# An mLSTM cell feeding a two-matrix block: first weight staged in unused activation columns, q scaling on GpSimd, tanh moved into the mix

## The chip, the core and the metric

The kernel runs on one core of one Trainium2 chip. The metric is device time in microseconds (us) of one execution. The five engines are TensorE (PE; its weight loads are shown as PEld), VectorE (DVE), ScalarE (ACT), GpSimd (POOL) and SyncE (SP, here the engine that issues nearly all transfers). Each runs its own list of instructions in order and waits for the others by semaphores.

## The reference

For 4 batches x 8 heads, a gated recurrent cell runs over 768 positions with head size 40. Its result is brought to 3072 tokens x 320, and goes through two matrices with a leaky ReLU between them:

```python
for t in range(S):
    m_new = np.maximum(f_gate[:, :, t] + m, i_gate[:, :, t])
    f_stab = np.exp(f_gate[:, :, t] + m - m_new)
    i_stab = np.exp(i_gate[:, :, t] - m_new)
    C = f_stab[..., None, None] * C + i_stab[..., None, None] * np.einsum('bhd,bhe->bhde', vt, kt)
    n = f_stab[..., None] * n + i_stab[..., None] * kt
    h_tilde = np.einsum('bhde,bhe->bhd', C, qt)
    denom = np.maximum(np.abs(np.einsum('bhd,bhd->bh', n, qt)[..., None]), 1.0)
    y[:, :, t] = sigmoid(o_gate[:, :, t]) * h_tilde / denom
x = y.transpose(0, 2, 1, 3).reshape(3072, 320)
h = x @ w_in                              # 320 x 2048
out = np.maximum(0.01 * h, h) @ w_out     # 2048 x 320
```

The two weights arrive as 64-bit floats; all else is float32.

## The kernel before, in words

**Chunks and steps.** Time is cut into six chunks of 128 positions. A step s handles one chunk of one batch, s = 4 x chunk + batch, so there are 24 steps. Inside a chunk the recurrence is a masked product: scores between the keys and queries of the chunk, weighted by gates, plus the state C carried from the chunk before.

**What a step does** (the letters in brackets are used in the prediction):

- `ahead(s)` prepares it. `prep_kq` (L398) transposes keys and queries on DVE into `kqT` (L403), and multiplies the queries by a decay `ea` (L409, two instructions of 40x512) into `qs`, which lies in the `kq` tile. `prep_mask` (L357) adds the causal mask to the 128x1024 tile `w` on POOL. `prep_exp` (L365) takes eight exponentials of `w` on ACT. `prep_vu` (L384) scales values on POOL. `prep_o` (L392) takes the tanh of the o gate on ACT.
- `u_scores(s)` (L432) multiplies keys and queries on PE; DVE multiplies the scores into `w` (L436).
- `u_mix(s)` updates the state and computes the output: PE writes `pT` from C and `qs` (L507) and from `w` and the values (L513); DVE transposes it into `hb` (L519), forms denominators, and multiplies by the gate (L523, which needs the tanh); POOL divides (L526); DVE adds to the state (L465) and transposes the result `x` (L530). The sync engine writes `x` to DRAM (L533) and `gather_x` reads it back in the layout that the matrix block needs (L547).

`ahead(s+1)` is emitted right after `u_scores(s)`, and `u_mix(s)` some units later.

**The matrix block.** While the steps of chunk c run, PE also multiplies the tokens of chunk c-1. Per chunk there are eight pairs: each writes two PSUM tiles `ph` with `w_in` (L576; 20 records in the trace for each pair, the first 12 from `first`, 8 from `second`), and ACT applies the leaky ReLU to both (L584), which also frees them. Then sixteen parts multiply by `w_out` (L611, 8 records each). For chunk 0 each pair is cut into two halves of 256 tokens. The tiles `ph` and the output tiles `po` come from one PSUM pool of four buffers, so a pair can only start when the ReLU of the pair two before it has read its tiles.

**Who sets the order.** PE, DVE, ACT and POOL run exactly in the order in which the Python code emits their instructions. A loop over the units of the matrix block (L761 to L791) puts the units of the steps between them. The sync engine's list is ordered by the scheduler of the framework, and each transfer also waits for the one that used its semaphore before: there are eight of these in turn, shared by the queues of SP and ACT.

**Weights.** Each of the eight blocks of the two weights (n = 0 to 3 for `w_in`, 4 to 7 for `w_out`) lands as 64-bit words in a `raw` tile of a pool with two buffers and is then narrowed: an Abs on ACT (L209) and six instructions on DVE (L211 to L227). Block 0 has no `raw` tile: it lands in the last columns of `acts`, the tile of the activations, which chunk 0 does not fill until later. The o gates of the first four steps lie in such columns too.

**Chunk 1** is the stage where the narrowing of blocks 2 to 7, the steps of chunk 1 and the matrix block of chunk 0 run together: `todo` (L751) says at which unit i the narrowing of each block starts; `lead` (L758) delays the first scores to i = 11.

Of the kernel before, what the change touches and what calls it, by code (L numbers as in the profile page):

```python
# [11 lines left out]
U64 = mybir.dt.uint64  # L12
# [6 lines left out]
def kernel(  # L19
# [26 lines left out]
    nc = tc.nc  # L46
# [5 lines left out]
    Dm, FF = moe_w_in.shape  # L52
# [9 lines left out]
    NF = FF // P  # L62
    GT = B * P
# [55 lines left out]
    acts_l = acts[:].rearrange("p f t -> p (f t)")  # L119
# [26 lines left out]
    QN = NF // 4  # L146
    QC = 4 * P
    WC = KC * 2 * P
# [12 lines left out]
    def run_of(r, at):  # L161

        ks = SLOTS[r][at:]
        return ks[0], next((i for i in range(1, len(ks)) if ks[i] != ks[i - 1] + 2), len(ks))
# [4 lines left out]
    def load_weights(n):  # L169

        if n < QN:
            dst = w_in[:, n, :]
        else:
            dst = w_out[:, 4 * (n - QN) : 4 * (n - QN + 1), :].rearrange("p a d -> p (a d)")
        to = dst
        if wide:
            if n == 0:
                raw = acts_l[:, NF * GT - 2 * WC :].bitcast(U64)
            else:
                raw = wk.tile([P, dst.shape[1]], U64, name="raw")[:]  # L180
            raws[n] = (raw, dst)
            to = raw
        if n < QN:
            for r in range(2):
                cols = slice(n * QC + 2 * P * r, n * QC + 2 * P * (r + 1))
                src = moe_w_in[:, cols].rearrange("(k p) c -> p k c", p=DP)
                half = to[DP * r : DP * (r + 1), :].rearrange("p (k c) -> p k c", k=KC)
                at = 0
                while at < KC:
                    k0, n_k = run_of(r, at)  # L190
                    nc.sync.dma_start(half[:, at : at + n_k, :], src[:, k0 : k0 + 2 * n_k - 1 : 2, :])  # L191
                    at += n_k
        else:
            rows = moe_w_out[(n - QN) * QC : (n - QN + 1) * QC, :]
            nc.sync.dma_start(to.rearrange("p (a d) -> p a d", d=Dm), rows.rearrange("(a p) d -> p a d", p=P))
# [101 lines left out]

    def load_o(s):
        c, b = divmod(s, B)
        at = NF * GT - 2 * WC - (s + 1) * Dm  # L300
        st[s]["o"] = acts_l[:, at : at + Dm]
        nc.sync.dma_start(
            st[s]["o"].rearrange("p (h d) -> p h d", d=D), o_gate[b, :, ts(c, P), :].rearrange("h p d -> p h d"),
        )
# [14 lines left out]
    def raw_blocks(s, i, w):  # L319

        return blocks(rb_t[s % NR][:, i, QW : QW + RL])[:, :, :w]
# [67 lines left out]
    def prep_o(s):  # L389

        o = st[s]["o"] if s < B else raw_blocks(s, 2, DB)
        nc.scalar.activation(o, o, AF.Tanh, scale=0.5)  # L392
# [5 lines left out]
    def prep_kq(s):  # L398

        d = st[s]  # L400
        d["kqT"] = wk.tile([P, 2, PR * P], F32, name="kqT")
        for i in range(2):
            nc.vector.transpose(  # L403
                in_blocks(d["kqT"][:, i]), raw_blocks(s, i, QW).rearrange("p (j n) d -> p j n d", n=TB),
            )
        d["qs"] = d["kq"][:, 1].rearrange("p h d -> p (h d)")
        for r in range(2):
            rows = slice(DP * r, DP * r + D)
            nc.vector.tensor_tensor(  # L409
                d["qs"][rows], d["kqT"][rows, 1], d["ea"][rows].rearrange("p j t -> p (j t)"), op=ALU.mult,  # L410
            )

# [85 lines left out]
    def u_mix(s):  # L498

        c, b = divmod(s, B)  # L500
        d = st[s]
        if c + 1 < NB:
            state(s)
        pT = psc.tile([P, PR * P], F32, name="pT", tag="c")
        for j in range(PR):
            for r in range(2):
                nc.tensor.matmul(  # L507
                    pT[DP * r : DP * (r + 1), ts(j, P)], lhsT=C[:, b, j, r, :], rhs=d["qs"][:, ts(j, P)],
                    start=True, stop=False,
                )  # L510
            for r in range(2):
                h = 2 * j + r
                nc.tensor.matmul(  # L513
                    pT[DP * r : DP * (r + 1), ts(j, P)], lhsT=d["va"][:, h], rhs=d["w"][:, h, :], start=False, stop=True,
                )
        if c + 1 < NB:
            state_scale(s)
        hb = wk.tile([P, PR * TB, QW], F32, name="hb", bufs=1)
        nc.vector.transpose(hb[:].rearrange("p (j n) d -> p j n d", n=TB), in_blocks(pT[:]))  # L519
        den = wk.tile([P, PR * TB], F32, name="den")  # L520
        denominators(den[:], hb[:, :, DB])
        x3 = xb[:, :, :DB]
        nc.vector.scalar_tensor_tensor(  # L523
            x3, in0=raw_blocks(s, 2, DB), scalar=1.0, in1=hb[:, :, :DB], op0=ALU.add, op1=ALU.mult,
        )
        nc.gpsimd.tensor_tensor(x3, x3, den[:].unsqueeze(2).to_broadcast([P, PR * TB, DB]), op=ALU.mult)  # L526
        if c + 1 < NB:
            state_add(s)
        xq = wk.tile([P, PR * P], F32, name="x")
        nc.vector.transpose(in_blocks(xq[:]), xb[:].rearrange("p (j n) d -> p j n d", n=TB))  # L530
        to = x_dr[s].rearrange("(j n i) t -> n i j t", n=4, i=DB)
        for n in range(4):
            nc.sync.dma_start(to[n], xq[QW * n : QW * n + DB].rearrange("p (j t) -> p j t", t=P))  # L533
        del st[s]

    def gather_x(s):

        c, b = divmod(s, B)
        if ("xT", c) not in st:
            st["xT", c] = wk.tile([P, KC, GT], F32, name="xT", bufs=1)  # L540
        xT = st["xT", c]
        src = x_dr[s].rearrange("(k p) t -> p k t", p=DP)
        for r in range(2):
            at = 0
            while at < KC:
                k0, n = run_of(r, at)
                nc.sync.dma_start(xT[DP * r : DP * (r + 1), at : at + n, ts(b, P)], src[:, k0 : k0 + 2 * n - 1 : 2, :])  # L547
                at += n
# [91 lines left out]
    def ahead(s):  # L640

        if s < NS:
            prep_kq(s)
            if s + NR < NS:
                load_blocks(s + NR, 0)
                load_blocks(s + NR, 1)
            prep_mask(s)
            prep_exp(s)
            prep_vu(s)
            prep_o(s)  # L650

    def feed(s):
        load(s)
# [80 lines left out]
    with tc.manual_schedule(engines={E.PE, E.DVE, E.Activation, E.Pool}):  # L734
        ffs = first_chunk()
        feed(B)
        for i in range(3):
            load_blocks(B, i)
        load_weights(QN)
        load_weights(QN + 1)  # L740
        feed(B + 1)
        for i in range(3):
            load_blocks(B + 1, i)
        load_weights(QN + 2)
        load_weights(QN + 3)
        feed(B + 2)
        feed(B + 3)


        ffs = ffs[4:6] + ffs[2:4] + ffs[6:]  # L750
        todo = {0: 2, 4: 3, **{9 + 4 * n: QN + n for n in range(4)}}  # L751
        now = iter(())
        for c in range(1, NB + 1):
            if c > 1:
                ffs = ff_units(c - 1)
            cells = cell_units(c) if c < NB else []
            n_ff, n_c = len(ffs), len(cells)
            lead = 10 if c == 1 else 0  # L758
            done = 0
            waiting = []  # L760
            for i in range(n_ff):  # L761
                if c == 1:
                    if i in todo:
                        for _ in now:
                            pass
                        now = narrow_weights(todo[i])
                    next(now, None)
                    next(now, None)
                    if i == 8:
                        u_gates(1)  # L770
                        ahead(B)
                if i == lead and c + 1 < NB:
                    bus[c + 1] = gates(c + 1)
                ffs[i]()
                upto = min(n_c, max(0, i + 1 - lead) * n_c // (n_ff - 6 - lead))
                while done < upto:
                    fn, s = cells[done]
                    fn(s)
                    done += 1
                    if fn is u_scores:  # L780
                        ahead(s + 1)
                    elif fn is u_mix:
                        waiting.append(s)
                        if s + NR < NS:
                            load_blocks(s + NR, 2)
                        if s + NL < NS:
                            feed(s + NL)
                if i >= n_ff // 2 - 1:
                    for s in waiting:
                        gather_x(s)  # L790
                    waiting.clear()  # L791


# [29 lines left out]
```

## Time and profile before

| | |
|---|---|
| time, median of 3 runs | 611.62 us (611.05 to 612.6) |
| span of the profiled execution | 611.2 us |
| PE busy | 545.6 us, 89% |
| DVE busy | 257.3 us, 42% |
| ACT busy | 154.9 us, 25% |
| POOL busy | 110.8 us, 18% |
| transfers | 69.89 MB, mean 114 GB/s |

PE is busy nine tenths of the span, so what counts is where it is not: before about 63 us, in chunk 1 (63 to 190 us), and shortly where one chunk follows another. From 190 us on each chunk takes about 87 to 90 us. In the timelines a bracket at the end of a line says how long the engine had been idle and what ended that; "issue" means that the profile shows no cause.

### The profile page before, as it was taken

Reading aid. Unit: us, or ns where it says so; the run is one execution under the profiler, and the core shown is the slowest. Engines: PE = TensorE matmul, PEld = TensorE weight load, DVE = VectorE, ACT = ScalarE, POOL = GpSimd, SP = SyncE. Lnnn points to the kernel's source line nnn. Section 1 sums busy time; section 2 is a strip of 40 time slices with the busy share of each in tenths; the row PEclk is TensorE's granted clock in tenths of the full one; section 3 lists DMA queues with packets and bytes.
Section 4 is the critical chain, followed back from the end, with each engine's and each line's share of the span. In section 5 each row is a group of like instructions: output and inputs, shape, how many; then the busy total and the mean of one; then the engine's idle time right before and its main releaser. Section 6 shows DMA issues by size and latency. Waiting matters only on the chain.

```text
span 611.2 us, 9093 instructions
## 1 busy us (share of the span) xinstructions
PE 545.6 (89%) x3428; PEld 375.2 (61%) x3428; DVE 257.3 (42%) x423; ACT 154.9 (25%) x401; POOL 110.8 (18%) x128
## 2 busy tenths in 40 slices
PE   5876992978655999998999989999989999999997
PEld 5765882756435656675557758557757567754575
DVE  4756796698830555242444423543503433100000
ACT  4443442420202332203321203330203330012100
POOL 4021520333020322130333020332100110000000
PEclk9998895999786999999999998999999999999999
DMA  9995588744574454661564660664650231100000
GB/s 141 169 170 125 122 254 188 177 159 106 137 174 125 108 137 129 151 157 59 139 149 117 153 160 11 149 144 122 153 146 25 71 92 38 48 23 1 0 23 21
DMA packets 158412, 69.89 MB, mean 114 GB/s; under 512 B 87072, under 2 KB 151200, under 8 KB 158368
## 3 DMA queue, kind: packets, MB, share of 16 engines
q1 hardware_dynamic: 157696, 69.08, 47.8%
q8 instruction: 27, 0.44, 0.3%
q10 hardware_dynamic: 672, 0.23, 0.2%
q14 instruction: 17, 0.14, 0.1%
HBM read 61.90 MB, written 7.37 MB: 113 GB/s over the span
## 4 chain that ended last, share of the span: by engine, by line
PE 72%; SPq 9%; DMA 6%; DVE 6%; issue 5%; ACT 1%; POOL 0%; ACTq 0%; DVEq 0%; POOLq 0%
PE ph L576 34%; PE po L611 28%; PE pT L513 3%; SPq L296 3%; PE pT L507 3%; SPq L314 3%; PE sc L432 3%; DMA rb<-in_k_dram 2%; SPq L191 1%; DVE kqT L403 1%; DVE kq L409 1%; PE dC L444 1%; DMA a_dr<-a 1%; DMA raw<-in_moe_w_in_dram 1%; SPq L331 1%
## 5 line engine op out<-in xcount | busy, mean ns | idle before, releaser
L576 PE MATMUL ph<-xT,w_in 64*128 64x512 f32 (+1 forms) x1120 | 228.0, 557 | 33.9 <-issue 16.3
L611 PE MATMUL po<-w_out,acts 128*128 128x320 f32 x768 | 214.8, 436 | 3.6 <-DVE w_out L227 3.6
L576 PEld LDWEIGHTS ph<-xT,w_in 64*128 64x128 f32 x1120 | 132.6, 199 | 113.1 <-issue 85.5
L611 PEld LDWEIGHTS po<-w_out,acts 128*128 128x128 f32 x768 | 143.5, 190 | 67.4 <-issue 6.0
L584 ACT ACTIVATE acts<-ph 128x512 f32<-128x512 f32 (+1 forms) x112 | 53.7, 532 | 160.7 <-PE ph L576 150.8
L436 DVE TENSOR_TENSOR w<-w,sc 128x512 f32<-128x512 f32 x48 | 30.7, 682 | 149.5 <-PE sc L432 149.5
L365 ACT ACTIVATE w<-w,gT 128x128 f32<-128x128 f32 x192 | 58.5, 394 | 17.5 <-POOL w L357 17.4
L455 POOL TENSOR_TENSOR C<-C,gL 64x168 f32<-64x168 f32 x32 | 15.8, 495 | 240.9 <-PE pT L507 239.7
L616 ACT COPY y<-po 128x320 f32<-128x320 f32 x24 | 10.2, 425 | 194.4 <-PE po L611 166.5
L357 POOL TENSOR_TENSOR w<-w,cmask 128x1024 f32<-128x1024 f32 x20 | 47.4, 2372 | 0.1
L513 PE MATMUL pT<-w,va 128*64 128x128 f32 x320 | 34.5, 280 | 8.2 <-issue 5.7
L403 DVE STREAM_TRANSPOSE kqT<-rb 128x512 f32<-128x512 f32 x40 | 41.1, 1105 | 0.0
L519 DVE STREAM_TRANSPOSE hb<-pT 128x512 f32<-128x512 f32 x20 | 14.3, 716 | 60.5 <-PE pT L513 60.5
L526 POOL TENSOR_TENSOR xb<-xb,den 128x320 f32<-128x320 f32 x20 | 14.6, 728 | 111.0 <-DVE xb L523 94.8
L507 PE MATMUL pT<-kq,C 128*64 128x128 f32 x320 | 34.0, 283 | 0.0
L432 PEld LDWEIGHTS sc<-kqT 40*128 40x128 f32 x384 | 28.4, 205 | 8.1 <-issue 7.4
L409 DVE TENSOR_TENSOR kq<-kqT,ea 40x512 f32<-40x512 f32 x40 | 29.4, 736 | 4.6 <-DMA ea<-a_dr 3.3
L432 PE MATMUL sc<-kqT 40*128 40x128 f32 x384 | 30.5, 297 | 0.0
L513 PEld LDWEIGHTS pT<-w,va 128*64 128x64 f32 x320 | 23.7, 141 | 9.4 <-issue 6.7
L530 DVE STREAM_TRANSPOSE x<-xb 128x512 f32<-128x512 f32 x20 | 22.4, 1120 | 8.3 <-POOL xb L526 8.3
L507 PEld LDWEIGHTS pT<-kq,C 128*64 128x64 f32 x320 | 21.8, 140 | 2.4 <-issue 2.0
L392 ACT ACTIVATE rb<-rb 128x320 f32<-128x320 f32 x20 | 9.3, 465 | 43.9 <-DMA rb<-in_o_gate_dram 39.9
(84 smaller groups left out, 278.7 us busy)
## 6 DMA issues: line engine op xcount, KB each, us to landing
w<-a_dr SPq DMA_DIRECT2D x20, 512.0 KB
rb<-in_k_dram SPq DMA_DIRECT2D x80, 80.0 KB
rb<-in_q_dram SPq DMA_DIRECT2D x80, 80.0 KB
rb<-in_o_gate_dram SPq DMA_DIRECT2D x80, 80.0 KB
ea<-a_dr SPq DMA_DIRECT2D x40, 128.0 KB
raw<-in_moe_w_out_dram SPq DMA_DIRECT2D x4, 1280.0 KB
kq<-in_k_dram SPq DMA_DIRECT2D x24, 160.0 KB
xT<-x_dr SPq DMA_DIRECT2D x40, 96.0 KB
```

The source lines that it names most:

```text
L357: nc.gpsimd.tensor_tensor(w[:], w[:], cmask[:].unsqueeze(1).to_broadcast([P, H, P]), op=ALU.add)
L365: nc.scalar.activation(w[:, h, :], w[:, h, :], AF.Exp, bias=gT[c][:, 0, bh : bh + 1], scale=1.0)
L403: nc.vector.transpose(in_blocks(d["kqT"][:, i]), raw_blocks(s, i, QW).rearrange("p (j n) d -> p j n d", n=TB),)
L409: nc.vector.tensor_tensor(d["qs"][rows], d["kqT"][rows, 1], d["ea"][rows].rearrange("p j t -> p (j t)"), op=ALU.mult,)
L432: nc.tensor.matmul(sc[r][:, j, :], lhsT=kqT[rows, 0, ts(j, P)], rhs=kqT[rows, 1, ts(j, P)], start=True, stop=True,)
L436: nc.vector.tensor_tensor(w[:, r::2, :], w[:, r::2, :], sc[r][:], op=ALU.mult)
L507: nc.tensor.matmul(pT[DP * r : DP * (r + 1), ts(j, P)], lhsT=C[:, b, j, r, :], rhs=d["qs"][:, ts(j, P)], start=True, stop=False,)
L513: nc.tensor.matmul(pT[DP * r : DP * (r + 1), ts(j, P)], lhsT=d["va"][:, h], rhs=d["w"][:, h, :], start=False, stop=True,)
L530: nc.vector.transpose(in_blocks(xq[:]), xb[:].rearrange("p (j n) d -> p j n d", n=TB))
L576: nc.tensor.matmul(ph[r][:, cols], lhsT=w_row(r, slot, j), rhs=xT[DP * r : DP * (r + 1), slot, cols], start=(slot == 0), stop=(slot == KC ...
L584: nc.scalar.activation(acts[:, f, cols], ph[r][:, cols], AF.Prelu, alpha=0.01)
L611: nc.tensor.matmul(po[n][:], lhsT=acts[:, f, ts(n, P)], rhs=w_out[:, f, :], start=(f == 0), stop=(f == NF - 1),)
```

## The change

Four edits:

1. Block 1 of the weights lands in unused columns of `acts` too, below block 0; the first o gates move further down. This leaves both `raw` buffers free for blocks 2 and 3 at once.
2. The loads of `w_out` (blocks 4 to 7) are no longer issued among the transfers of chunk 1's steps. Each is issued in the loop when the narrowing of the block before it starts, so that chunk 1's own transfers go ahead of them instead of waiting in one queue behind a load that waits for a buffer.
3. The tanh of the o gate moves from `ahead(s+1)` to the head of `u_mix(s)`, so that ACT does not stand waiting for a gate that is not needed yet. With it, `gather_x` is emitted before the transfers for later steps (`feed`, `load_blocks`).
4. The scaling of the queries by `ea` moves from DVE to POOL, which has more room.

```diff
         if wide:
-            if n == 0:
-                raw = acts_l[:, NF * GT - 2 * WC :].bitcast(U64)
+            if n < 2:
+                at = NF * GT - 2 * WC * (n + 1)
+                raw = acts_l[:, at : at + 2 * WC].bitcast(U64)
...
-        at = NF * GT - 2 * WC - (s + 1) * Dm
+        at = NF * GT - 4 * WC - (s + 1) * Dm
...
-            nc.vector.tensor_tensor(
+            nc.gpsimd.tensor_tensor(
                 d["qs"][rows], d["kqT"][rows, 1], d["ea"][rows].rearrange("p j t -> p (j t)"), op=ALU.mult,
             )
...
         d = st[s]
+        prep_o(s)
         if c + 1 < NB:
             state(s)
...
             prep_vu(s)
-            prep_o(s)
...
             load_blocks(B, i)
-        load_weights(QN)
-        load_weights(QN + 1)
         feed(B + 1)
...
             load_blocks(B + 1, i)
-        load_weights(QN + 2)
-        load_weights(QN + 3)
         feed(B + 2)
...
                         now = narrow_weights(todo[i])
+                        if QN - 1 <= todo[i] < 2 * QN - 1:
+                            load_weights(todo[i] + 1)
...
-                        if s + NR < NS:
-                            load_blocks(s + NR, 2)
-                        if s + NL < NS:
-                            feed(s + NL)
                 if i >= n_ff // 2 - 1:
                     for s in waiting:
                         gather_x(s)
                     waiting.clear()
+                while fed < done:
+                    fn, s = cells[fed]
+                    fed += 1
+                    if fn is u_mix:
+                        if s + NR < NS:
+                            load_blocks(s + NR, 2)
+                        if s + NL < NS:
+                            feed(s + NL)
```

More of the change, by code (lines that the diff above doesn't have):

```diff
@@ L758 @@
             lead = 10 if c == 1 else 0
-            done = 0
+            done = fed = 0
             waiting = []
@@ L783 @@
                         waiting.append(s)
+                if i >= n_ff // 2 - 1:
+                    for s in waiting:
+                        gather_x(s)
+                    waiting.clear()
+                while fed < done:
+                    fn, s = cells[fed]
+                    fed += 1
+                    if fn is u_mix:
                         if s + NR < NS:
@@ L787 @@
                             feed(s + NL)
[L788 to L791, printed above, removed]
 _INS = ['q', 'k', 'v', 'i_gate', 'f_gate', 'o_gate', 'moe_w_in', 'moe_w_out']
```

## The prediction, made before the changed kernel had run

> **What bounds the kernel now.** I read the busy shares first, then the waits, then the timeline of each engine where PE stands still. The shares say PE:
>
> ```profile
> PE 545.6 (89%) x3428; PEld 375.2 (61%) x3428; DVE 257.3 (42%) x423; ACT 154.9 (25%) x401; POOL 110.8 (18%) x128
> PEclk9998895999786999999999998999999999999999
> ```
>
> The second line is the granted clock in 40 slices of 15.3 us: it falls where PE had stood still. PE's timeline from 70 to 200 us shows the long holes, all in chunk 1:
>
> ```profile
> 104.62 6.44 PE L576 MATMUL ph<-xT,w_in 64*128 64x256 f32 x40 [12.00 <-ACT acts L584]
> ...
> 158.85 1.09 PE L513 MATMUL pT<-w,va 128*64 128x128 f32 x3 [5.70 <-issue]
> ...
> 189.54 9.26 PE L576 MATMUL ph<-xT,w_in 64*128 64x512 f32 x32 [13.67 <-issue]
> ```
>
> The first is ACT standing at the gate loads of L91, behind transfers queued late on SP; the second is ACT at a tanh whose o gate came late (15.76 us idle in front of it); the third is the last gather of x, issued late by SP. From 190 us on there are no holes but three at chunk boundaries (1.65, 2.63, 2.87 us). In a middle step (s = 9) the timelines of PE, ACT, POOL and DVE read:
>
> ```profile
> 215.86 6.18 PE L576 MATMUL ph<-xT,w_in 64*128 64x512 f32 x28
> 221.97 0.67 PE L444 MATMUL dC<-vu,kq 128*64 128x42 f32 x16
> 224.33 7.14 PE L576 MATMUL ph<-xT,w_in 64*128 64x512 f32 x32
> ```
>
> ```profile
> 213.56 2.44 ACT L365 ACTIVATE w<-w,gT 128x128 f32<-128x128 f32 x8
> 217.67 0.47 ACT L392 ACTIVATE rb<-rb 128x320 f32<-128x320 f32 x1 [1.67 <-DMA rb<-in_o_gate_dram]
> 218.05 1.07 ACT L584 ACTIVATE acts<-ph 128x512 f32<-128x512 f32 x2
> 222.07 1.09 ACT L584 ACTIVATE acts<-ph 128x512 f32<-128x512 f32 x2 [2.95 <-PE ph L576]
> ```
>
> ```profile
> 210.83 2.36 POOL L357 TENSOR_TENSOR w<-w,cmask 128x1024 f32<-128x1024 f32 x1
> ```
>
> ```profile
> 216.13 1.29 DVE L436 TENSOR_TENSOR w<-w,sc 128x512 f32<-128x512 f32 x2 [4.10 <-PE sc L432]
> 217.33 2.08 DVE L403 STREAM_TRANSPOSE kqT<-rb 128x512 f32<-128x512 f32 x2
> 219.44 1.40 DVE L409 TENSOR_TENSOR kq<-kqT,ea 40x512 f32<-40x512 f32 x2
> ```
>
> The reader should see that POOL masks w of step 10 at 210.8, before the scores of step 9 (215), so ACT's eight exponentials run at 213.6 and the ReLU at 218.05 follows its pair (8 records after 215.86, done at 217.6) at once. PE never waits for it.
>
> **The Trainium skill.** "GPSIMD Engine Reference", section 3.1, puts a two-input `tensor_tensor` at about 2.6 cycles an element, 4497 ns for 2048 elements; the trace agrees: the 128x1024 mask takes 2357 ns, 2.3 ns an element. "TensorE: Matmul & The Clock Gate", Part 1, says ScalarE, VectorE and GpSimd take their instructions strictly first in, first out, and that PE falls to half clock after an idle window of about 3.4 us, free-running. The trace agrees roughly: 32 records of L576 take 7.07 us; after the 1.65 us hole 7.21; after 2.63 us 10.38; after 2.87 us 40 records take 10.63 for 8.84.
>
> **The change part by part.**
>
> *Block 1 in `acts`.* Nothing: ACT's Abs of block 1 (48.1 us) has no wait in front of it before. Up to 82.4 us PE's order is the same and runs without a hole from 62.7; the o gates only change address.
>
> *q scaling on POOL.* Two 40x512 at 2.3 ns an element plus a little: 1.2 us each, 2.4 a step (DVE took 1.4). Bounds: 0.8 each at the page's best loop of 1.8 cycles, 1.35 if DVE contends (the 128x336 of L384 goes from 0.77 to 1.35). The sum, 48 us on an engine 18% busy, is no matter; the place is. In the built program POOL has: L409(s+1), mask(s+1), vu(s+1), then C(s), xb(s). L409(s+1) needs `kqT(s+1)`, which DVE makes after L436(s), which needs PE's scores of s. So the mask, independent of all this before, now waits for the scores. Behind the mask on ACT stand exp(s+1), and behind that the ReLUs; PE waits for those through the four PSUM buffers. At s = 9: DVE done 219.4; POOL 2.4 gives 221.9; mask 2.36, 224.2; exp 2.45, 226.7; ReLU of that pair frees its first tile at 227.2, the second at 227.7. The pair that needs these starts at 224.33 before: 3.1 us of standing. At s = 8 the same sum, from scores at 198.7 and kqT at 202.9, gives 210.7 to 211.2 against 208.0: 2.9 us. In chunks 2, 3 and 4 two steps each stand so (the third's ReLU is needed only in the last quarter of a part, some 12 us later, just in time): 6 x 3.0 = 18 us. In chunk 5 the scores stand a pair later; L409 to ReLU ends about 0.7 us late, twice: 1.4.
>
> *Clock.* Each such hole is about 2.8 us. Holes of that size cost 0.14, 3.3 and 1.8 us of slower matmuls on top; I take their mean, 1.75: 6 x 1.75 = 10.5. Ends: 0 and 3.3 each.
>
> *tanh in the mix.* ACT's tanh(s) now stands behind exp(s+1) and, in the middle steps, two ReLUs. DVE's L523 waits for it some 3 us, hidden, since the next thing that needs DVE is scores 6 us later. At chunk ends x is ready 2.5 us later, but its gather is issued right after the write and two loads, not behind eight transfers; the gather comes 0.2 to 1.4 us earlier than before: -0.5 a boundary, -1.5 for three.
>
> *Chunk 1 with the loads moved.* The transfers of step 5 are now there by 70 us, and the gate loads of L91 do not stand, so the 12.0 us hole goes. In its place: kqT(4) ends at 85.3 as before, then POOL 87.7, mask 90.1 (before: 70.9), exp 92.5, ReLU 93.1. PE has filled its four buffers at 87.1 and stands 6.0 us. Abs of block 4 moves from 86.5 to 93.1, and its narrowing with the gates of chunk 2 (8.5 us on DVE) ends at 103.1; L436(4), kqT(5) 106.4; POOL 108.8, mask 111.1, exp(5) 113.5, ReLU 114.1, and only then a buffer for the first part: 114.1 against 113.36 before. The 12 us are gone again. Going on with the same durations: L436(5) 124.5, L436(6) 139.2, kqT(7) 141.3, POOL's L409(7) 143.7. Now SP: its load of `ea` for step 8 waits for that L409. Behind it in the new order stand `ea`, a load, gather(4), write of x(5), gather(5) with its landing, and six or seven loads, about 13 us at 0.45 to 0.6 each, and then the load of the last `w_out` block: issued at about 157, before at 127.7. It lands in about 5 us (packets of the four before: 5 us each): Abs at 162.5 (before 152.7), four DVE instructions 4.1, L436(7) 169.3 (before 159.3). Then kqT(8) 171.4, POOL 173.8, `ea(9)` on SP, 12 us of issue to the write of x(7) at 186, its gather 189 to 191.6, PE about 194: 4.5 us later than 189.54. I take +5, ends -5 (the last block earlier) and +10.
>
> Sum: 5 + 18 + 10.5 + 1.4 - 1.5 = 33.4; 611.6 + 33.4 = 645.0 us.
>
> **Rivals.**
> - *Chunk 1 pays as meant.* The 12.0 and 5.7 us holes go, SP keeps up, and the standing in chunks 2 to 5 is there, with little clock loss: 611.6 - 13 + 19.4 + 3 = 621. For it: those holes are real and their causes are removed. Against: the sum above, row by row.
> - *Faster.* The ReLUs are not held: POOL or ACT is further ahead than I read, or PE has slack. Then 12.0 + 5.7 + part of 13.67, some 20 us, is won: 592. For it: POOL is 18% busy. Against: order on POOL and ACT is fixed, and the mask stands behind L409.
> - *All gains and losses meet*: 611. It needs chunk 1 to win about 20 us and no clock loss.
> - *Clock at its worst*: 3.3 us a hole and chunk 1 at +10: 645 + 9.3 + 5 = 659.
>
> **How the numbers follow.** The forecast 0.60, chunk 1 paying 0.16, clock at its worst 0.12, faster 0.09, meeting 0.03. The low end leaves out the clock loss (-10.5) and takes chunk 1 at -5 (-10): 624, opened to 621 for the first rival; the high end is the last rival, 660. Faster 0.09, same 0.03, slower 0.88.
>
> **What would show it.** In the changed profile: POOL's mask right behind L409, each after kqT; ACT idle in front of L365, released by POOL, in nearly every step; ReLU waits that are no longer PE's; PE holes of about 3 us after the mix of steps 8, 9, 12, 13, 16 and 17, released by L584, with 32 records over 7.2 us behind them; the hole at 92 us gone, one at 87 us in its place; the last `w_out` load issued past 150 us. I am wrong if ACT's exp does not wait for POOL, or if the chunks from 190 us on still take 87 us; and wrong on chunk 1 if chunk 2 starts before 185 us.

## The result: slower by 6.9%, and the profile after

The changed kernel takes 654.59 us (median of four runs, 652.15 to 657.96) against 612.11 for the kernel before on the same chip: a ratio of 1.069, 95% interval 1.064 to 1.075. The forecast was 645.0, range 621 to 660. In the profiled executions the span grows from 611.2 to 652.4 us, by 41.2.

The page of the changed kernel, shares, granted clock and two of its costliest groups (busy us, mean ns of one, then the idle time in front and what ended most of it):

```profile
PE 565.5 (87%) x3428; PEld 403.1 (62%) x3428; DVE 227.5 (35%) x383; ACT 153.9 (24%) x401; POOL 167.2 (26%) x168
PEclk9997989879586997999997999898999999999999
...
L410 POOL TENSOR_TENSOR kq<-kqT,ea 40x512 f32<-40x512 f32 x40 | 57.3, 1433 | 277.4 <-DVE kqT L404 258.5
L366 ACT ACTIVATE w<-w,gT 128x128 f32<-128x128 f32 x192 | 58.6, 388 | 215.4 <-POOL w L358 188.2
```

POOL took over 57 us of work and is still only 26% busy; DVE lost 30 us of work. Nothing in the busy shares says that this should cost anything. The idle columns do: POOL now stands 258.5 us in front of the scaling, waiting for DVE's `kqT`, and ACT stands 188.2 us in front of the exponentials, waiting for POOL's mask. That PE has *more* busy time (565.5 for 545.6) with the same 3428 matmuls is its clock: from the sixteenth slice on four are below 9, where the kernel before has one.

Where the 41 us are is read from the times at which each chunk's matrix block starts on PE (the first instruction of 64x512 that writes `ph` in chunk 2, and so on):

| kernel | chunk 2 starts | chunk 2 | chunk 3 | chunk 4 | chunk 5 |
|---|---|---|---|---|---|
| before | 189.5 | 87.9 | 87.1 | 90.4 | 83.9 |
| after | 205.7 | 98.4 | 95.6 | 95.6 | 84.7 |

So 16.2 us come from before chunk 2, and 10.5, 8.5, 5.2 and 0.8 from the chunks after it: 41.2. PE's timeline of the changed kernel (start, length, what, and in brackets how long PE had stood and what ended that) shows both parts:

```profile
93.79 7.13 PE L578 MATMUL ph<-xT,w_in 64*128 64x256 f32 x40 [5.78 <-ACT acts L586]
...
114.90 4.53 PE L613 MATMUL po<-w_out,acts 128*128 128x320 f32 x8 [5.54 <-ACT acts L586]
...
178.33 1.09 PE L515 MATMUL pT<-w,va 128*64 128x128 f32 x3 [17.57 <-issue]
...
205.72 7.86 PE L578 MATMUL ph<-xT,w_in 64*128 64x512 f32 x20 [9.48 <-issue]
...
229.64 7.18 PE L578 MATMUL ph<-xT,w_in 64*128 64x512 f32 x31 [2.85 <-ACT acts L586]
249.38 10.51 PE L578 MATMUL ph<-xT,w_in 64*128 64x512 f32 x32 [2.86 <-ACT acts L586]
323.65 9.22 PE L578 MATMUL ph<-xT,w_in 64*128 64x512 f32 x32 [2.80 <-ACT acts L586]
344.99 10.49 PE L578 MATMUL ph<-xT,w_in 64*128 64x512 f32 x32 [2.85 <-ACT acts L586]
```

Once chunk 2 has started, PE stands six times for 2.80 to 2.87 us, twice each in chunks 2, 3 and 4, always for the ReLU (L586). The two in chunk 4, at 419 and 440 us, look the same (2.87 and 2.85, with 9.15 and 10.45 us of matmuls behind them). Where there is no hole, 32 such records take 7.14 us; behind the six holes they take about 0, 3.4, 2.1, 3.4, 2.0 and 3.3 us longer. In chunk 1 the old hole of 12.0 us is gone, but holes of 5.78 us at 88 us and 5.54 at 109 stand in its place, both for the ReLU, and the 5.7 us hole in front of the last mix has become 17.57.

### The profile page after: what moved, and what is told of

It is laid out like the page before. It is cut to its first block, busy times and chain, and to the rows that moved or that the text cites. A ratio compares the mean times of both kernels' runs of the same rounds, so it can differ in the third digit from the quotient of the medians.

```text
span 652.4 us, 9151 instructions
## 1 busy us (share of the span) xinstructions
PE 565.5 (87%) x3428; PEld 403.1 (62%) x3428; DVE 227.5 (35%) x383; ACT 153.9 (24%) x401; POOL 167.2 (26%) x168
## 4 chain that ended last, share of the span: by engine, by line
PE 43%; issue 28%; POOL 9%; DMA 5%; ACT 5%; DVE 4%; SPq 4%; ACTq 0%; POOLq 0%; DVEq 0%
PE po L613 22%; PE ph L578 16%; POOL kq L410 6%; ACT w L366 4%; DMA ea<-a_dr 3%; SPq L297 2%; POOL w L358 2%; PE sc L433 2%; PE pT L509 1%; PE pT L515 1%; POOL xb L528 1%; DMA rb<-in_k_dram 1%; SPq L315 1%; PE dC L445 1%; DMA va<-in_v_dram 1%
## 5 line engine op out<-in xcount | busy, mean ns | idle before, releaser
L578 PE MATMUL ph<-xT,w_in 64*128 64x512 f32 (+1 forms) x1120 | 244.6, 576 | 35.5 <-ACT acts L586 24.3
L613 PE MATMUL po<-w_out,acts 128*128 128x320 f32 x768 | 217.9, 441 | 8.4 <-ACT acts L586 5.5
L578 PEld LDWEIGHTS ph<-xT,w_in 64*128 64x128 f32 x1120 | 156.9, 206 | 106.6 <-issue 56.3
L613 PEld LDWEIGHTS po<-w_out,acts 128*128 128x128 f32 x768 | 145.0, 192 | 73.7 <-issue 7.8
L410 POOL TENSOR_TENSOR kq<-kqT,ea 40x512 f32<-40x512 f32 x40 | 57.3, 1433 | 277.4 <-DVE kqT L404 258.5
L366 ACT ACTIVATE w<-w,gT 128x128 f32<-128x128 f32 x192 | 58.6, 388 | 215.4 <-POOL w L358 188.2
L586 ACT ACTIVATE acts<-ph 128x512 f32<-128x512 f32 (+1 forms) x112 | 52.7, 528 | 91.8 <-PE ph L578 91.5
L358 POOL TENSOR_TENSOR w<-w,cmask 128x1024 f32<-128x1024 f32 x20 | 48.3, 2414 | 1.6
L521 DVE STREAM_TRANSPOSE hb<-pT 128x512 f32<-128x512 f32 x20 | 14.3, 714 | 84.1 <-PE pT L515 84.1
L433 PEld LDWEIGHTS sc<-kqT 40*128 40x128 f32 x384 | 31.4, 204 | 6.6 <-issue 5.6
L433 PE MATMUL sc<-kqT 40*128 40x128 f32 x384 | 33.1, 298 | 0.0
L525 DVE SCALAR_TENSOR_TENSOR xb<-rb,hb 128x320 f32<-128x320 f32 x20 | 9.8, 489 | 44.5 <-ACT rb L393 37.5
L445 PEld LDWEIGHTS dC<-vu,kq 128*64 128x64 f32 x320 | 12.1, 150 | 9.8 <-POOL kq L410 5.9
```

The costliest lines, as they stand in the source:

```text
L358: nc.gpsimd.tensor_tensor(w[:], w[:], cmask[:].unsqueeze(1).to_broadcast([P, H, P]), op=ALU.add)
L366: nc.scalar.activation(w[:, h, :], w[:, h, :], AF.Exp, bias=gT[c][:, 0, bh : bh + 1], scale=1.0)
L410: nc.gpsimd.tensor_tensor(d["qs"][rows], d["kqT"][rows, 1], d["ea"][rows].rearrange("p j t -> p (j t)"), op=ALU.mult,)
L433: nc.tensor.matmul(sc[r][:, j, :], lhsT=kqT[rows, 0, ts(j, P)], rhs=kqT[rows, 1, ts(j, P)], start=True, stop=True,)
L578: nc.tensor.matmul(ph[r][:, cols], lhsT=w_row(r, slot, j), rhs=xT[DP * r : DP * (r + 1), slot, cols], start=(slot == 0), stop=(slot == KC ...
L586: nc.scalar.activation(acts[:, f, cols], ph[r][:, cols], AF.Prelu, alpha=0.01)
```

## Why the last mix of chunk 1 waits 17.57 us

POOL in chunk 1, scaling (L410) and mask (L358) of four steps:

```profile
107.03 2.65 POOL L410 TENSOR_TENSOR kq<-kqT,ea 40x512 f32<-40x512 f32 x2 [15.32 <-DVE kqT L404]
109.76 2.34 POOL L358 TENSOR_TENSOR w<-w,cmask 128x1024 f32<-128x1024 f32 x1
127.35 4.90 POOL L410 TENSOR_TENSOR kq<-kqT,ea 40x512 f32<-40x512 f32 x2 [6.71 <-DVE kqT L404]
...
144.91 4.19 POOL L410 TENSOR_TENSOR kq<-kqT,ea 40x512 f32<-40x512 f32 x2 [5.96 <-DVE kqT L404]
149.18 3.47 POOL L358 TENSOR_TENSOR w<-w,cmask 128x1024 f32<-128x1024 f32 x1
```

DVE's last narrowing instruction (L228, two tensors in, 128x1280) of three blocks in the same stretch:

```profile
102.33 1.49 DVE L228 TENSOR_TENSOR w_out<-w_out,wm 128x1280 f32<-128x1280 f32 x1
...
128.63 2.48 DVE L228 TENSOR_TENSOR w_out<-w_out,wm 128x1280 f32<-128x1280 f32 x1
...
150.49 3.52 DVE L228 TENSOR_TENSOR w_out<-w_out,wm 128x1280 f32<-128x1280 f32 x1
```

Alone, two scalings take 2.65 us and the narrowing 1.49; side by side they take 4.90 and 2.48, or 4.19 for the scalings, and a mask beside L228 takes 3.47 where it takes 2.34. Each holds up the other. The Trainium skill names this: "GPSIMD Engine Reference", section 1, has POOL's SBUF interfaces shared with VectorE, with contention where the DVE instruction has two SBUF inputs, as L224 and L228 have, or runs in a 2-port performance mode. The trace agrees, with a factor of 1.6 to 1.85 on a scaling. L222 has only one tensor in and still took 1.79 us beside the scaling at 144.91, where it takes 0.83; whether it runs in such a mode no run here shows.

The ends of the instructions fit two engines that take turns, a whole instruction at a time: the mask at 149.18 ends at 152.65, and L228, begun at 150.49, ends 1.36 us after that, close to the 1.49 it takes alone. The kernel before has the same without any scaling on POOL. Its POOL (a mask, and the `prep_vu` of L384, which elsewhere takes 0.77):

```profile
68.21 2.65 POOL L357 TENSOR_TENSOR w<-w,cmask 128x1024 f32<-128x1024 f32 x1
...
118.40 2.02 POOL L384 TENSOR_TENSOR vu<-va,gT 128x336 f32<-128x336 f32 x1
```

and its DVE beside them:

```profile
68.68 2.87 DVE L221 TENSOR_SCALAR wm<-w_in 128x1280 uint32<-128x1280 uint32 x1
...
117.13 2.66 DVE L219 SCALAR_TENSOR_TENSOR w_out<-raw,wm 128x1280 uint32<-128x1280 uint32 x1
```

L221 takes 0.83 us alone; here it ends at 71.55, 0.69 after the mask. L384 ends at 120.42, 0.63 after L219. No run here tries the pair by itself.

Behind that, SP's list (its load of `ea`, L332, waits for the scaling that reads the old one):

```profile
149.13 1.25 SPq L332 DMA_DIRECT2D ea<-a_dr  x2
...
163.17 0.43 SPq L196 DMA_DIRECT2D raw<-in_moe_w_out_dram  x1
...
203.15 2.54 SPq L549 DMA_DIRECT2D xT<-x_dr  x4
```

In the kernel before, the load of the last `w_out` block left some 35 us earlier:

```profile
127.74 0.40 SPq L195 DMA_DIRECT2D raw<-in_moe_w_out_dram  x1
```

It leaves at 163.17 for two reasons. It is now emitted later, which alone does not account for all: in the run below that differs only in having the scaling on DVE it leaves at 142.33. And it stands in SP's list behind the `ea` that waits for POOL. ACT waits 16.68 us for it, starts its Abs at 172.18, and since DVE's narrowing stands in front of the scores of step 7 on DVE, the mix of step 7 and the last gather (203.15) come late.

## The experiments

One table first; each run had its own runs of the kernel before on the same chip (612.15 to 612.95 us). Starts and lengths of chunks are in us, as above.

| run | time | ratio (95%) | chunk 2 starts | chunks 2, 3, 4, 5 |
|---|---|---|---|---|
| changed, scaling on DVE | 597.02 | 0.974 (0.968 to 0.980) | 181.2 | 89.1, 84.1, 84.1, 81.9 |
| changed, mask ahead of scaling | 607.48 | 0.992 (0.988 to 0.995) | 192.3 | 91.3, 84.1, 84.2, 81.9 |
| before, scaling on POOL | 665.26 | 1.085 (1.077 to 1.092) | 202.3 | 101.7, 99.1, 97.3, 87.3 |
| before, tanh in the mix | 616.72 | 1.006 (1.004 to 1.009) | 192.9 | 88.6, 88.8, 89.2, 84.0 |
| before, first weight and loads | 608.41 | 0.993 (0.991 to 0.996) | 189.0 | 87.9, 87.0, 88.0, 84.0 |
| before, gather ahead | 602.30 | 0.983 (0.979 to 0.987) | 187.2 | 89.0, 84.1, 84.1, 81.9 |
| scaling on DVE, last load earlier | 589.46 | 0.962 (0.958 to 0.966) | 176.9 | 89.0, 84.1, 84.1, 81.9 |
| mask ahead, last load earlier | 595.02 | 0.972 (0.968 to 0.976) | 181.8 | 88.8, 84.1, 84.1, 81.9 |
| and last x from ACT | 595.16 | 0.972 (0.967 to 0.977) | 167.8 | 101.7, 84.1, 84.1, 81.9 |
| and first y from ACT | 595.99 | 0.974 (0.966 to 0.981) | 182.3 | 88.0, 84.1, 84.1, 81.9 |
| and both from ACT | 582.72 | 0.951 (0.945 to 0.958) | 171.9 | 86.9, 84.1, 84.1, 81.9 |

The "and" rows start from the row "scaling on DVE, last load earlier".

### The place of the scaling

Undo it in the changed kernel:

```diff
-            nc.gpsimd.tensor_tensor(
+            nc.vector.tensor_tensor(
                 d["qs"][rows], d["kqT"][rows, 1], ...
```

> The change with its fourth part undone: the queries are scaled on DVE again, the rest stays. Theory (the mask behind the scaling on POOL holds exp and ReLU): no PE hole behind the mixes of chunks 2 to 4, these chunks at 84 to 88 us instead of 95 to 98, chunk 2 starting before 192 us, 591 to 603 us in all. Rival (the moved loads, the moved tanh or the new order on SP cost the time): six holes of about 2.85 us or other holes stay, 630 us or more.

597.02 us, in the theory's range: the six holes are gone and chunks 3 and 4 take 84.1, less than before's 87.1 and 90.4 (chunk 2, at 89.1, is a little over the 88 expected). Chunk 2 starts at 181.2, earlier than before. So the scaling on POOL cost 57.6 us in this kernel (654.59 - 597.02), and the other edits together win 15.6 (612.64 - 597.02).

Leave it on POOL, but emit the mask first:

```diff
         if s < NS:
+            prep_mask(s)
             prep_kq(s)
...
-            prep_mask(s)
             prep_exp(s)
```

> The whole change, but with the mask emitted ahead of the query scaling, both on POOL. Theory (the place in POOL's order, not the work): the holes of chunks 2 to 4 go as with the scaling on DVE, 592 to 606 us, although POOL is as busy as in the change. Rival (POOL is too slow for this work, or its contention with DVE is the cost): chunks 2 to 4 stay at 93 us or more, 635 us or more.

607.48 us, 1.5 above the theory's range, but the six holes go entirely: chunks 3 and 4 take 84.1 and 84.2 with all scalings still on POOL. The profile page of this run, in the same two groups:

```profile
L410 POOL TENSOR_TENSOR kq<-kqT,ea 40x512 f32<-40x512 f32 x40 | 57.9, 1447 | 242.1 <-DVE kqT L404 232.7
L366 ACT ACTIVATE w<-w,gT 128x128 f32<-128x128 f32 x192 | 58.5, 393 | 18.7 <-POOL w L358 18.5
```

POOL still waits 232.7 us in front of L410, but ACT's wait for the mask falls from 188.2 to 18.5. This run separates place from speed. From chunk 2 on POOL is fast enough; what cost 5.7 us of standing and 3.4 to 5.4 of slower matmuls a chunk was that an instruction whose input comes late stood ahead of one whose input was there. "TensorE: Matmul & The Clock Gate", Part 1, says that these engines take their instructions first in, first out, and this run is that sentence in numbers: the same instructions, one order with the six holes, the other without them. In chunk 1 the order does not do as much: chunk 2 starts at 192.3, where it starts at 181.2 with the scaling on DVE. There POOL's time counts as well, and the slow scalings beside the narrowing are in it (4.89, 4.22 and 4.88 us a step in this run).

The scaling on POOL alone, in the kernel before:

```diff
-            nc.vector.tensor_tensor(
+            nc.gpsimd.tensor_tensor(
```

> The kernel before with only the query scaling moved to POOL. Theory: six holes of 2.8 to 2.9 us in chunks 2 to 4, released by the ReLU, with up to 3.4 us of slower matmuls behind each; 635 to 650 us. Rival (it takes the other three parts to lose the time): 609 to 616 us.

665.26 us: the direction is right, the size is not; it costs 52.6 us by itself, 15 beyond the theory's range. PE's timeline of this run, two holes of chunk 2:

```profile
224.91 9.04 PE L576 MATMUL ph<-xT,w_in 64*128 64x512 f32 x32 [3.28 <-ACT acts L584]
246.49 10.20 PE L576 MATMUL ph<-xT,w_in 64*128 64x512 f32 x32 [3.26 <-ACT acts L584]
```

Each hole is 0.4 us longer than in the changed kernel, which fits one tanh (0.47 us) that here still stands on ACT between the exponentials and the ReLU. Its span is 48.9 us longer than that of the kernel before: 12.8 of these lie ahead of chunk 2, where the theory had put nothing, and 19.6 are the six holes. Unlike the changed kernel it also keeps the holes at the chunk boundaries.

### The other edits, one at a time

> The kernel before with only the tanh moved into the mix. Theory: the 5.7 us hole of chunk 1 goes, nothing else changes, since exp is not late here: 603 to 611 us. Rival (the tanh, now late in ACT's order, delays x and with it the gather at each chunk boundary): boundaries 2 us longer each, 614 to 620 us.

```diff
     def u_mix(s):
...
+        prep_o(s)
...
-            prep_o(s)
```

616.72 us: a miss. The theory wanted 603 to 611, since ACT no longer stands for the o gate. The number lies in the rival's range, but not for the rival's reason: the boundary holes are 2.08, 2.57 and 3.04 us, and chunks 2 to 5 together take about 1.3 us more, not 6. The hole in front of the last mix did shrink, from 5.70 to 3.27 us, but the next one grew. PE's timeline of this run:

```profile
156.51 1.09 PE L514 MATMUL pT<-w,va 128*64 128x128 f32 x3 [3.27 <-issue]
...
192.95 9.47 PE L577 MATMUL ph<-xT,w_in 64*128 64x512 f32 x32 [19.70 <-issue]
```

And SP's:

```profile
152.52 0.75 SPq L328 DMA_DIRECT2D w<-a_dr  x1
...
160.68 1.25 SPq L331 DMA_DIRECT2D ea<-a_dr  x2
...
188.24 2.54 SPq L548 DMA_DIRECT2D xT<-x_dr  x4
```

SP stands from 153.3 to 160.7 us for the scaling that frees `ea`, with the gather of step 5 now behind that load; in the kernel before it stood ahead. Moving the tanh also moved what the scheduler puts into SP's list, and 13.67 us of standing for the gather became 19.70.

> The kernel before with only the loads changed (block 1 in the columns of the activations, the loads of the second weight issued in the loop). Theory: the 12.0 us hole at 92 us goes, but the last block lands late and PE stands 14 us or more at the mix of step 7; chunk 2 starts at 182 to 190 us, the boundaries stay: 604 to 613 us. Rival (the moved loads pay in full): chunk 2 at 178 us or earlier, 600 us or less.

```diff
+            if n < 2:
+                at = NF * GT - 2 * WC * (n + 1)
...
-        load_weights(QN)
-        load_weights(QN + 1)
...
+                        if QN - 1 <= todo[i] < 2 * QN - 1:
+                            load_weights(todo[i] + 1)
```

608.41 us, as expected (the hole at the mix of step 7, put at 14 us or more, is 13.79). The 12.0 us hole falls to 2.5, and 8.1 of these 9.5 us are given back in front of the last mix, which now waits 13.79 us where it waited 5.70: the first weight and the loads trade one late transfer for another.

> The kernel before with only the gather of x emitted ahead of the transfers of later steps. Theory: the chunk boundaries lose their holes (1.65, 2.63, 2.87 us) and the slow matmuls behind them (up to 3.3 us), so chunks 2 to 4 take 84 to 86 us instead of 87 to 90, and chunk 2 starts 3 to 5 us earlier: 596 to 604 us. Rival (the boundaries wait for x itself, not for SP's order): 609 to 613 us.

```diff
                         waiting.append(s)
+                if i >= n_ff // 2 - 1:
+                    for s in waiting:
+                        gather_x(s)
+                    waiting.clear()
+                while fed < done:
...
                             load_blocks(s + NR, 2)
...
-                if i >= n_ff // 2 - 1:
-                    for s in waiting:
-                        gather_x(s)
-                    waiting.clear()
```

602.30 us, as expected. Chunk 2 alone is not as forecast: it starts 2.3 us earlier, not 3 to 5, and takes 89.0, not 84 to 86. Chunks 3, 4 and 5 take 84.1, 84.1 and 81.9: the boundary holes of the kernel before go altogether, and with them the slow matmuls behind them. This edit alone is worth 9.8 us, and it is the one for which the prediction took off 1.5.

### The last load of the second weight

In the run with the scaling on DVE the largest hole was again in front of the last mix. PE's timeline:

```profile
156.95 1.09 PE L515 MATMUL pT<-w,va 128*64 128x128 f32 x3 [15.66 <-issue]
...
181.18 6.86 PE L578 MATMUL ph<-xT,w_in 64*128 64x512 f32 x20 [7.11 <-issue]
```

and ACT waited 25.7 us for that load. It was issued at 142.33. The next two kernels emit it one narrowing earlier, once with the scaling on DVE and once with it on POOL behind the mask:

```diff
-                        if QN - 1 <= todo[i] < 2 * QN - 1:
+                        if QN - 1 <= todo[i] <= QN + 1:
                             load_weights(todo[i] + 1)
+                        if todo[i] == QN + 1:
+                            load_weights(2 * QN - 1)
```

> The queries scaled on DVE, the rest of the change kept, and the load of the last block of the second weight emitted one narrowing earlier, so that on SP it stands ahead of the decay of step 8 instead of behind the gather of step 5. Theory (that load's place is what chunk 1 still pays: PE stood 15.66 us at the mix of step 7 in the run with the scaling on DVE): that hole falls under 4 us, chunk 2 starts at 168 to 176 us instead of 181, the chunks after are unchanged, 583 to 592 us. Rival (chunk 1 is bound by DVE or by SP's count of transfers): the hole moves to the gather, chunk 2 starts at 179 us or later, 595 us or more.

> Queries scaled on POOL, the mask emitted ahead of it, and the load of the last block of the second weight emitted one narrowing earlier. Theory (in chunk 1 the scaling on POOL runs against a busy DVE and takes 2.4 us an instruction instead of 1.3, and SP's load of the next decay waits for it): also faster by the load, 592 to 601 us, but some 6 to 11 us behind the same kernel with the scaling on DVE. Rival (the place of the scaling no longer matters once the mask is ahead and the load is early): within 3 us of that kernel.

589.46 and 595.02 us, both in their ranges (chunk 2 starts at 176.9 in the first, just past the 168 to 176 expected). PE in the first of them:

```profile
147.78 0.40 PE L515 MATMUL pT<-w,va 128*64 128x128 f32 x2 [3.27 <-ACT rb L393]
...
176.91 8.04 PE L578 MATMUL ph<-xT,w_in 64*128 64x512 f32 x20 [12.04 <-DMA xT<-x_dr]
```

The load leaves at 118.82, the hole falls from 15.66 to 3.27. Of these 12.4 us, 4.9 come back as a longer wait for the gather (7.11 to 12.04); the time falls by 7.6. The second kernel has the scaling on POOL and the mask ahead of it, and is 5.6 us slower, a little under the 6 to 11 expected; 4.9 of it are there at the start of chunk 2. That is what the scaling on POOL still costs in chunk 1 once the mask no longer stands behind it. The slow scalings are part of it: beside the narrowing they take 4.85, 4.17 and 4.87 us a step there too. How much of the 5.6 they make up was not measured apart.

### What then holds chunk 2

> The kernel of e5_last_load_early with the write and the gather of step 7's x (the last pair of chunk 1) issued by ACT in place of SP. Theory: the 12.04 us hole of TensorE before chunk 2 in e5 is there because SP issues its transfers without a pause from 151.8 us on, so that the write leaves only at 171.6 and the gather at 174.3; from ACT they leave earlier, chunk 2 starts at 165 to 171 us in place of 176.9, later chunks are as in e5, and the time is 578 to 585. Rival: ACT's own queue of work, or what the transfers wait for, holds them as long: chunk 2 at 176 us or later, and 588 or more.

```diff
+        eng = nc.scalar if s == 2 * B - 1 else nc.sync
-            nc.sync.dma_start(to[n], ...
+            eng.dma_start(to[n], ...
```

595.16 us: half a miss. The gather left at 159.5 (from SP: 174.3) and chunk 2 started at 167.8, as the theory had it, and the gain was lost 19 us later. PE's timeline:

```profile
167.75 6.94 PE L580 MATMUL ph<-xT,w_in 64*128 64x512 f32 x20 [4.57 <-issue]
187.10 5.41 PE L580 MATMUL ph<-xT,w_in 64*128 64x512 f32 x12 [12.41 <-ACT y L620]
```

ACT's:

```profile
186.62 0.83 ACT L620 COPY y<-po 128x320 f32<-128x320 f32 x2 [23.69 <-DMA out_dram<-y]
```

The next pair needs PSUM buffers that hold `po`; ACT copies these into `y`, which has to be stored first, and these stores stand in SP's list at 181.7 us. So the last two runs issue the four stores of chunk 0's `y` from ACT, alone and with the edit above:

```diff
-                nc.sync.dma_start(out[n * S + g * P : n * S + (g + 1) * P, :], y[:])
+                (nc.scalar if g == 0 else nc.sync).dma_start(out[...], y[:])
```

> The kernel of e5_last_load_early with the four stores of y of chunk 0 issued by ACT right behind each copy, in place of SP. Theory: in e5 the y tiles come free late but the gather of x sets the start of chunk 2, so only the small hole behind that start goes: chunk 2 at 175 to 178 us, 585 to 589. Rival: the stores on ACT take semaphores that SP's transfers wait for, and the gather comes later: chunk 2 past 180 us, 592 or more.

> The kernel of e9_last_x_on_act with the four stores of y of chunk 0 issued by ACT too. Theory: in e9 chunk 2 started at 167.75 us, 9.2 earlier than in e5, but PE then stood 12.41 us for two y tiles whose stores stand late in SP's list (181.7 us); with these stores on ACT that hole goes to 3 us or less and the gain stays: 579 to 584. Rival: the hole only moves, to the gates of chunk 2 or the scores of step 8, whose transfers also stand late in SP's list: a hole of 6 us or more before 215 us, and 588 or more.

Alone it makes the kernel slower, 595.99: the rival. SP's waits and PE's timeline of that run:

```profile
SPq L315 <- DMA out_dram<-y: 6.6, 3, 4.5
```

```profile
182.31 10.64 PE L578 MATMUL ph<-xT,w_in 64*128 64x512 f32 x31 [20.62 <-issue]
```

SP's transfers at L315, those of q above all, stood 6.6 us (three waits, the longest 4.5) behind stores that ACT had issued, and the gather left 5.6 us later than without them (179.93 for 174.34). With both edits the time is 582.72 us, inside the theory's 579 to 584. PE's timeline:

```profile
171.95 9.50 PE L580 MATMUL ph<-xT,w_in 64*128 64x512 f32 x31 [6.92 <-DMA fi<-in_i_gate_dram]
```

Chunk 2 starts 4.2 us later than with the gather alone on ACT, and there is no hole of a microsecond or more in the rest of it. SP waits 0.9 us for such stores and 5.1 (the longest 4.5) for the writes of x that ACT issues, but the last gather no longer stands in SP's list behind these waits. Two edits that each cost 6 us win 7 together: the gather on ACT needs `y` stored early, and the stores on ACT hold up SP's list, which no longer has the last gather in it.

This is the fastest kernel of the study, 4.9% under the kernel before.

## Why the prediction was right, point by point

**The main step held.** The mask stood behind the scaling, the exponentials behind the mask, the ReLU behind these; PE stood six times, behind the predicted mixes of chunks 2 to 4. Holes of 3.0 us each were forecast, 17.1 us in all were found for 18. The run with the mask first shows the cause: the same work in another order has no holes.

**The sum was right partly by luck.** It said +33.4, the spans say +41.2: the terms of chunk 1 and of the boundaries were off in opposite ways, by about 11 and 7 us. To split the chunks, I take as clean lengths the 84.1 us that chunks 3 and 4 have, and the 81.9 that chunk 5 has, in the runs without holes.

| term | forecast | measured |
|---|---|---|
| chunk 1 | +5 | +16.2 |
| six holes | +18 | +17.1 |
| slow matmuls behind them | +10.5 | about +14 |
| chunk 5 | +1.4 | +2.8 (84.7 less 81.9) |
| boundaries | -1.5 | about -9 (what is left of 41.2) |

*Chunk 1* was forecast hole by hole, and its first half came true: 6.0 us forecast at 87 us, 5.78 measured; ReLU at 93.1, measured 93.4; the first part at 114.1, measured 114.9. The step that was mis-sized is the one after it, "POOL's L409(7) 143.7" with 2.4 us for two scalings: beside the narrowing they take 4.2 to 4.9, outside the bounds given (1.35 each), and this one ended at 149.1, 5.4 us late. Of these, 3.5 us came with kqT(7), done at 144.8 where 141.3 was forecast; the scaling of the step before, which took 4.90, stands ahead of it by way of the mask, the exponentials, the tanh and DVE's list. Another 1.8 are its own 4.19. The bound of 1.35 was one reading of L384; the same trace has L384 at 2.02 and L221 at 2.87, as shown above, so the larger cost could have been read there. The issue of SP behind it was sized well (13 us forecast, 14.0 measured), but the load landed 9 us after its issue, not 5 (ACT's Abs at 172.2 for 162.5). That is +9.7 of the 11.7 us by which chunk 2 came later than the forecast 194.

*Clock.* Three of the six holes cost 3.3 or 3.4 us on top, two about 2.0, one nothing. The mean is 2.4, where 1.75 was taken from three holes of the kernel before. One of those three was 1.65 us long and cost almost nothing; the two of 2.63 and 2.87 us have a mean of 2.55 by the forecast's own figures. The idle window that "TensorE: Matmul & The Clock Gate", Part 1, gives is about 3.4 us. Here holes of 2.8 to 2.9, shorter than that, were followed by slower matmuls five times in six.

*Boundaries.* The step "the gather comes 0.2 to 1.4 us earlier than before" was too small. With the gather emitted ahead, in a kernel that differs from the one before in nothing else, all three boundary holes and the slow clock behind them go: 9.3 us in chunks 3 and 4 and 2.0 in chunk 5. Together that is more than the 9 us of the table, which is a remainder and so also holds the slower beginning of chunk 2 in the changed kernel (7.86 us for 20 records at 205.72, where 20 of the clean 32 would take about 4.5).

*Tanh in the mix* was costed at nothing beyond that, with DVE's wait of some 3 us hidden. No PE hole of chunks 2 to 4 is traced to it, but in chunk 1 DVE's L525 stood 4.80 us for the tanh, at 137.59, in front of the scores of step 6, from which kqT(7) follows. By itself it costs 4.1 us, for the reason seen in SP's list; in the changed kernel the gather is emitted ahead as well.

**The rivals.** "Chunk 1 pays as meant" comes true only in part with the scaling on DVE: chunk 2 starts 8.3 us earlier, but the hole of 5.7 us grows to 15.66 there instead of going. "Faster" would have had the right direction without that one edit (597 for its 592). In the changed kernel POOL stands against both. "Clock at its worst" (659) ended nearer to the time than the forecast did (4 us from it, not 10), but not for its reason: the clock loss, about 14 us, lay between the forecast's 10.5 and that rival's 19.8, chunk 1 beyond both, and the boundaries gave back what neither had counted.

**What stays open.** That POOL and DVE take turns in the narrowing is read from starts and ends in several traces; it was not tried by itself. How chunk 1's 16.2 us divide between the slower scalings and the order on POOL and SP is followed along one chain, not measured piece by piece. Why holes of equal length cost 0, 2 or 3.4 us wasn't tried.

## What to carry to other kernels

An engine that is 18% busy is not free: ask which instruction the new one stands in front of, and whether its input comes later than that one's. If so, emit the independent one first; here this was worth 47 us with no work removed. When a list of transfers is the bound, an edit that speeds up one consumer shows its gain only once the next entry in the list has been moved too, so follow the longest hole from run to run before you judge an edit by its own time.

## What the runs showed of the hardware

- Two-input POOL instructions of 40x512 took 1.3 us alone and up to 2.42 beside DVE instructions of 128x1280. Of these, two-input ones went from 1.49 to as much as 3.52 and a one-input one from 0.83 to 2.87, both beside a 128x1024 mask. Starts and ends fit taking turns by whole instructions: 0.69 and 1.36 us from the end of the mask to the end of the DVE instruction begun beside it.
- In the changed kernel PE holes of 2.80 to 2.87 us were followed by 0 to 3.4 us of slower matmuls; five of six cost 2 us or more.
- Stores issued by ACT held up transfers of SP by 4.5 us at most at a time, although the two engines issue from lists of their own.
